# A planned transformer block with its gradients: another order of operations and other homes for the buffers

## The chip, the cores and the metric

The kernel runs on one core of a Trainium2 chip. The metric is the device time of one execution in microseconds (us); lower is better. TensorE is called PE here, VectorE DVE, ScalarE ACT, GpSimd POOL, and SyncE, which issues most transfers, SP.

## The reference

A pre-layernorm block with local attention and a feed-forward part, and then the gradients of its output for all seven inputs, with `grad_out` as the incoming gradient. x is 2048 x 512 in bf16, there are 32 heads of 16, each position attends to 8 positions at distances 0, 2, ... 14, and the feed-forward part is 1792 wide.

```python
def _A_ref(x, wqkv, wo):
    ...
    q, k, v = qkv[0], qkv[1], qkv[2]          # x @ wqkv, by heads
    idx = pos[:, None] - (jnp.arange(W) * dil)[None, :]     # W = 8, dil = 2
    ...
    logits = jnp.einsum("bhsd,bhswd->bhsw", q, kg) * scale
    logits = jnp.where(mask[None, None, :, :], logits, -1e9)
    attn = _softmax(logits, axis=-1)
    o = jnp.einsum("bhsw,bhswd->bhsd", attn, vg)
    return (lambda x, *d: x.transpose(*d))(o, 0, 2, 1, 3).reshape(B, S, D) @ wo

def _B_ref(x, w1, b1, w2, b2):
    h = _gelu(jnp.einsum("bsd,df->bsf", x, w1) + b1)
    return jnp.einsum("bsf,fd->bsd", h, w2) + b2

h = x + _A_ref(_layernorm(x), A_wqkv, A_wo)
h2 = h + _B_ref(_layernorm(h), B_w1, B_b1, B_w2, B_b2)

def reference(A_x, A_wqkv, A_wo, B_w1, B_b1, B_w2, B_b2, B_x, grad_out):
    _out, _vjp = jax.vjp(_f, A_x, A_wqkv, A_wo, B_w1, B_b1, B_w2, B_b2)
    return (_out, *_vjp(grad_out))
```

## The kernel before

**Chunks and stages.** The 2048 rows are worked in four chunks of 512. For each chunk there are three stages.

The first is the attention forward. A layernorm on DVE and ACT gives `ln1`; it is transposed to `ln1T`, multiplied by the q and k halves of wqkv (`wqk`, L802) and by `wv` (L819). For the logits DVE multiplies q with the shifted k, in products of 128 x 4096 elements (`prf`, L672), and PE sums each product over a head's 16 columns with matmuls that put out 32 partitions ("32-column sums", L679). After the softmax, the weighted sum over v works likewise: POOL gathers shifted rows (L661), DVE multiplies (`prbo`, L698), PE sums (`bsum`, L707), and ACT empties the bank into `ost` (the operation "sink", L712). `oT` is its transpose, and wo with the residual gives `h` (L910). A second layernorm gives `ln2`, which goes to memory and comes back transposed as `ln2T` (L559).

The second stage is the feed-forward part, forward and backward. ff1 (L948) makes 14 tiles f0 to f13 of 128 x 512, each in one PSUM bank; ACT empties each bank with the bias added into `xb` (L950), and a gelu over up to four tiles gives `gl` (L953). ff2 (L1004) sums over all 14 tiles, and DVE adds `h` (`h2s`). The derivative of the gelu is made in place by ACT (a square L968, a tanh L972) and DVE (L969 to L982). gg (L1029) multiplies grad_out by w2, tile by tile, each in a bank that DVE empties while it multiplies by the derivative (gh, L1031). ACT makes column sums of grad_out (`jkb`, L1020). gl2 (L1052) goes back through w1, and a layernorm backward gives the gradient of h. Tiles `gl` and gh are also transposed to rows and stored (`g_d`, `gh_d`), for the weight gradients.

The third stage is the attention backward: products and sums of the kind above for the gradients of the logits, v, q and k (`prb`, `prbv`, `prbq`, `prbk`, with gathers `Rv`, `Rq`, `Rk` on POOL), then gl1 (L1165) back through wqkv and the first layernorm backward, which reads `ln1` again (`ln1b`, L1158). The weight gradients (L1193, results `wgs`) read the stored rows back (`gw1in`, `gw2in`) in groups and run where PE is free and at the end.

**The order.** The function calls do not set the order. Each call to `op()` only records an operation with its engine, its buffers and its function in a list of 2029; every buffer, in SBUF or PSUM, is an entry in a list of 969. Then `schedule()` takes two tuples written out in the file: `TURN`, one global order of the 2029 operations, and `HOMES`, a place for each of the 969 buffers: a byte offset in SBUF, or a number from 0 to 7 of a PSUM bank of 512 fp32 columns.

```python
    if len(self.turn) == len(self.ops) and len(self.homes) == len(self.bufs):
        for b, h in zip(self.bufs, self.homes):
            b.home = h
        self.order = [self.ops[i] for i in self.turn]
```

`emit()` issues the operations in that order and gives each buffer its place. An engine carries out its own operations strictly in that order; between engines the program waits where data has to be ready, and also where a place is used again: who writes into a bank waits until the bank's last reader is done. So `HOMES` decides for whom a matmul waits beyond its data, and `TURN` decides what that reader has queued ahead of it on its engine. DMAs are operations of SP or POOL in the same order.

Of the kernel before, what the change touches and what calls it, by code (L numbers as in the profile page):

```python
# [14 lines left out]
ACT = mybir.ActivationFunctionType  # L15
# [412 lines left out]
def kernel(  # L428
# [410 lines left out]
    def p1_attn(c):  # L839
# [15 lines left out]
        op("ACT", 0.61, lambda: A.copy(out=m1h(), in_=m1()[64:128, :]), r=[m1], w=[m1h], tag="m1h")  # L855
        op("DVE", tt_us(512), lambda: V.tensor_tensor(out=m2(), in0=m1()[0:64, :], in1=m1h(), op=ALU.max), r=[m1, m1h], w=[m2], tag="m2")
        op("ACT", 0.61, lambda: A.copy(out=m2h(), in_=m2()[32:64, :]), r=[m2], w=[m2h], tag="m2h")
# [648 lines left out]
)  # L1506
NV = (0, 1, 2, 3)
N2D = ()
B2PE = ()
GB2PE = ()  # L1510
GWA = ()
B1PE = ()
P1_OFF, P3_OFF = 400.0, 0.0
KEEP = 2
RLQ = "SP"
FM1 = ()
FM2 = (0, 1, 2, 3)
EARLY = 1
# [38 lines left out]
```

## Time and profile before

| what | us |
| --- | --- |
| median of 3 runs | 604.17 |
| lowest and highest run | 602.34 and 605.82 |
| the profiled execution, its own time | 603.35 |
| the profiled execution, its span | 601.6 |
| PE, DVE, ACT, POOL busy in the span | 565.8, 492.1, 353.2, 86.6 |
| mean granted TensorE clock | 0.994 |

The span runs from the first to the last instruction; the time of an execution has a little more around it. The busy times are of one profiled execution. In the rows of a timeline stand the start, the duration, the engine, the line of the kernel and the operation with its tiles; what is in brackets at the end is how long the engine stood idle before it, and what ended that. "xN" is the number of instructions that a row holds.

### The profile page before, as it was taken

Reading aid. Unit: us, or ns where it says so; the run is one execution under the profiler, and the core shown is the slowest. Engines: PE = TensorE matmul, PEld = TensorE weight load, DVE = VectorE, ACT = ScalarE, POOL = GpSimd, SP = SyncE. Lnnn points to the kernel's source line nnn. Section 1 sums busy time; section 2 is a strip of 40 time slices with the busy share of each in tenths; the row PEclk is TensorE's granted clock in tenths of the full one; section 3 lists DMA queues with packets and bytes.
Section 4 is the critical chain, followed back from the end, with each engine's and each line's share of the span. In section 5 each row is a group of like instructions: output and inputs, shape, how many; then the busy total and the mean of one; then the engine's idle time right before and its main releaser. Section 6 shows DMA issues by size and latency. Waiting matters only on the chain.

```text
span 601.6 us, 9239 instructions
## 1 busy us (share of the span) xinstructions
PE 565.8 (94%) x3526; PEld 257.4 (43%) x3580; DVE 492.1 (82%) x644; ACT 353.2 (59%) x519; POOL 86.6 (14%) x89
## 2 busy tenths in 40 slices
PE   4999989889879999999999999999999999999997
PEld 2444433434324444444455343334444354444443
DVE  8799899899899989998774679999999998984500
ACT  4578989998993797679545231316535535165112
POOL 3120505021000001000000300223213322100000
PEclk9999999999889999999999999999999999999999
DMA  8258999999998978979997999898898997979312
GB/s 256 86 187 265 331 258 299 262 177 328 238 251 238 281 166 234 211 210 197 277 252 193 285 351 254 259 342 318 289 378 325 338 326 251 333 219 325 108 36 70
DMA packets 161067, 150.46 MB, mean 250 GB/s; under 512 B 110688, under 2 KB 147456, under 8 KB 156160
## 3 DMA queue, kind: packets, MB, share of 16 engines
q1 hardware_dynamic: 154688, 102.69, 63.4%
q0 software_dynamic: 6336, 47.19, 22.0%
q8 instruction: 28, 0.46, 0.3%
q14 instruction: 15, 0.12, 0.1%
HBM read 78.25 MB, written 42.77 MB: 201 GB/s over the span
## 4 chain that ended last, share of the span: by engine, by line
PE 68%; DMA 8%; ACT 7%; DVE 4%; issue 3%; POOL 1%; SPq 0%; DVEq 0%; ACTq 0%; POOLq 0%
PE ps L1193 24%; PE ps L1029 8%; PE ps L1052 7%; PE ps L1165 6%; PE ps L1004 5%; PE ps L948 5%; PE ps L707 4%; PE ps L1074 2%; DMA gw1in<-gh_d 2%; PE ps L722 2%; DMA goT<-in_grad_out_dram 2%; DMA ln2T<-ln 2%; DMA out_dram<-wgs 2%; DVE prbo L698 1%; ACT xb L950 1%
## 5 line engine op out<-in xcount | busy, mean ns | idle before, releaser
L1029 PE MATMUL ps<-goT,w2T 128*128 128x512 bf16 x219 | 56.9, 389 | 8.5 <-ACT ost L712 4.5
L948 PE MATMUL ps<-ln2T,w 128*128 128x512 bf16 x224 | 55.4, 387 | 3.0 <-DMA ln2T<-ln 2.0
L1193 PE MATMUL ps<-gw1in,ln2b 128*128 128x512 bf16 (+1 forms) x256 | 52.7, 353 | 1.2 <-DMA gw1in<-gh_d 1.2
L1004 PE MATMUL ps<-w,gl 128*128 128x512 bf16 x219 | 52.5, 380 | 0.4 <-ACT ost L712 0.2
L1052 PE MATMUL ps<-w1T,xb 128*128 128x512 bf16 x217 | 51.3, 380 | 0.5 <-issue 0.2
L1193 PE MATMUL ps<-gor,gw2in 128*128 128x512 bf16 x217 | 50.7, 380 | 0.5 <-issue 0.2
L1031 DVE SCALAR_TENSOR_TENSOR xb<-xb,ps 128x512 bf16<-128x512 bf16 x56 | 38.1, 684 | 12.6 <-PE ps L1029 11.8
L1165 PE MATMUL ps<-wqkvT,gqkvT 128*128 128x512 bf16 x183 | 43.3, 380 | 0.8 <-issue 0.5
L950 ACT ACTIVATE xb<-ps,b1c 128x512 bf16<-128x512 f32 x56 | 36.9, 688 | 9.3 <-PE ps L948 9.0
L698 DVE TENSOR_TENSOR prbq<-Rq,cfq 128x4096 bf16<-128x4096 bf16 x16 | 36.2, 2286 | 5.1 <-DMA Rq<-k_d,rowi 1.5
L672 DVE TENSOR_TENSOR prb<-got,vw 128x4096 bf16<-128x4096 bf16 x16 | 36.2, 2282 | 4.9 <-PE ps L679 3.1
L737 ACT ACTIVATE gyr<-ps,rstd 128x512 bf16<-128x512 f32 x32 | 22.0, 687 | 31.1 <-PE ps L1165 16.3
L698 DVE TENSOR_TENSOR prbk<-Rk,cfk 128x4096 bf16<-128x4096 bf16 x16 | 36.0, 2285 | 4.6 <-PE ps L707 3.7
L564 ACT CAST wgs<-ps 128x512 bf16<-128x512 f32 (+1 forms) x30 | 16.3, 561 | 38.8 <-PE ps L1193 38.8
L672 DVE TENSOR_TENSOR prf<-qt,kt 128x4096 bf16<-128x4096 bf16 x16 | 36.1, 2274 | 3.4 <-ACT kt L564 3.2
L698 DVE TENSOR_TENSOR prbo<-Ro,cfo 128x4096 bf16<-128x4096 bf16 x16 | 36.4, 2288 | 2.5 <-PE ps L707 1.4
L1029 PEld LDWEIGHTS <-w2T 128*128 128x128 bf16 x224 | 22.0, 99 | 35.6 <-issue 11.3
L698 DVE TENSOR_TENSOR prbv<-Rv,cfv 128x4096 bf16<-128x4096 bf16 x16 | 36.3, 2285 | 0.5 <-ACT wgs L564 0.4
L661 POOL DMA_INDIRECT Rq<-k_d,rowi x8 | 16.4, 2051 | 131.7 <-DMA out_dram<-gbs 106.3
L1193 PEld LDWEIGHTS <-ln2b 128*128 128x128 bf16 x256 | 23.6, 98 | 27.0 <-issue 7.7
L948 PEld LDWEIGHTS <-w 128*128 128x128 bf16 x224 | 21.5, 99 | 31.2 <-issue 7.7
L968 ACT ACTIVATE x<-xb 128x2048 bf16<-128x2048 bf16 (+1 forms) x16 | 27.0, 1690 | 11.7 <-DVE h2s L1006 6.0
(175 smaller groups left out, 1066.6 us busy)
## 6 DMA issues: line engine op xcount, KB each, us to landing
g_d<-xrg SPq DMA_DIRECT2D x12, 512.0 KB
gh_d<-xrh SPq DMA_DIRECT2D x12, 512.0 KB
gw2in<-g_d SPq DMA_DIRECT2D x3, 2048.0 KB
gw1in<-gh_d SPq DMA_DIRECT2D x3, 2048.0 KB
ln_d<-ln SPq DMA_DIRECT2D x8, 512.0 KB
w<-in_B_w_dram SPq DMA_DIRECT2D x2, 1792.0 KB
out_dram<-wgs SPq DMA_DIRECT2D x13, 256.0 KB
v_d<-tmv SPq DMA_DIRECT2D x8, 256.0 KB
```

Of the source, the lines that this page charges most:

```text
L672: op("DVE", tt_us(4096), lambda g=g, pr=pr: V.tensor_tensor(out=pr(), in0=ql()[:, g, :].unsqueeze(1).to_broadcast([P, W, 512]), in1=_sub(k ...
L698: V.tensor_tensor(out=pr().rearrange("p a j (d h) -> p a j d h", h=H), in0=_sub(R()[:, o0, 0:1], [[st, 2], [512, 4], [32, DH], [1, H]]), i ...
L707: T.matmul(ps()[32 * j:32 * j + 32, :], lhsT=S32[:], rhs=pr()[:, hf, j, :], start=(hf == 0), stop=(hf == 1), skip_group_check=True)
L948: T.matmul(ps(), lhsT=w1()[:, dc, f * P:(f + 1) * P], rhs=cols(ln2T[c], dc, c in FM2), start=(dc == 0), stop=(dc == DC - 1))
L950: op("ACT", act_us(512, 1), lambda f=f, ps=ps, xb=xb, f0=f0: A.activation(out=xb()[:, f - f0, :], in_=ps(), func=ACT.Identity, bias=b1c[:, ...
L968: op("ACT", act_us(N), lambda xb=xb, x2=x2: A.activation(out=fl(x2), in_=fl(xb), func=ACT.Square), r=[xb], w=[x2], tag="x2", slack=6000)
L1004: T.matmul(ps(), lhsT=d["g"][f // 4]()[:, f % 4, j * P:(j + 1) * P], rhs=w2()[:, f, :], start=(f == 0), stop=(f == FT - 1))
L1029: T.matmul(ps(), lhsT=w2T()[:, dc, f * P:(f + 1) * P], rhs=goT()[:, dc, :], start=(dc == 0), stop=(dc == DC - 1))
L1031: op("DVE", 0.70, lambda f=f, ps=ps, z=z, f0=f0: V.scalar_tensor_tensor(out=z()[:, f - f0, :], in0=z()[:, f - f0, :], scalar=1.0, in1=ps() ...
L1052: T.matmul(ps(), lhsT=d["d"][f // 4]()[:, f % 4, j * P:(j + 1) * P], rhs=w1T()[:, f, :], start=(f == 0), stop=(f == FT - 1))
L1165: T.matmul(ps(), lhsT=d["gqkv"]()[:, b, j * P:(j + 1) * P], rhs=wqkvT()[:, b, :], start=(i == 0 and b == ks[0]), stop=(i == 2 and b == ks[ ...
L1193: T.matmul(ps()[:, 0:N], lhsT=l, rhs=r, start=(n == 0), stop=(n == k - 1))
```

## The change

Three things change in the file; the list of recorded operations stays the same: 2029 operations and 969 buffers, in both.

- `TURN` is another order of the same 2029 operations. The median operation stands 10 places from where it stood, the mean 18.
- `HOMES` is another list: 716 of 969 buffers have another place, 307 of the 408 PSUM places among them.
- `p1_attn` gets a branch: for chunks in a new tuple `MD` two copies of the softmax's maximum between partitions would be DMAs of SP instead of copies of ACT. `MD` is empty.

The diff, with the two tuples cut to their first lines:

```diff
-        op("ACT", 0.61, lambda: A.copy(out=m1h(), in_=m1()[64:128, :]), r=[m1], w=[m1h], tag="m1h")
+        if c in MD:
+            op("SP", 0.5, lambda: SY.dma_start(out=m1h(), in_=m1()[64:128, :]), r=[m1], w=[m1h], dma=0.25, tag="m1h")
+        else:
+            op("ACT", 0.61, lambda: A.copy(out=m1h(), in_=m1()[64:128, :]), r=[m1], w=[m1h], tag="m1h")
...
-        op("ACT", 0.61, lambda: A.copy(out=m2h(), in_=m2()[32:64, :]), r=[m2], w=[m2h], tag="m2h")
+        if c in MD:
+            op("SP", 0.5, lambda: SY.dma_start(out=m2h(), in_=m2()[32:64, :]), r=[m2], w=[m2h], dma=0.15, tag="m2h")
+        else:
+            op("ACT", 0.61, lambda: A.copy(out=m2h(), in_=m2()[32:64, :]), r=[m2], w=[m2h], tag="m2h")
...
 TURN = (
-    41, 0, 5, 4, 3, 1, 2, 18, 9, 7, 25, 6, 24, 10, 12, 29, 19, 23, 30, 8, 22, 11, 26, 31, 34, 27, 35, 144, 39, 20, 28, 40, 33, 32, 147,
-    37, 36, 145, 38, 146, 48, 148, 265, 149, 49, 266, 42, 50, 263, 43, 150, 153, 51, 44, 152, 154, 52, 151, 76, 155, 158, 53, 45, 159, 46,
...
+    0, 5, 4, 2, 1, 3, 9, 18, 6, 25, 13, 10, 24, 7, 29, 17, 22, 30, 19, 23, 11, 20, 8, 26, 31, 21, 27, 35, 34, 39, 28, 32, 33, 40, 147, 37,
+    144, 38, 145, 48, 146, 49, 148, 263, 149, 42, 50, 265, 43, 150, 153, 51, 44, 154, 152, 45, 151, 41, 76, 52, 46, 53, 58, 78, 47, 156,
...
 HOMES = (
-    32192, 40384, 44480, 85440, 173760, 188096, 99776, 204480, 130624, 114112, 23936, 89536, 165568, 77248, 225088, 52672, 153152, 169664,
-    161472, 212672, 188096, 220992, 208576, 114112, 220992, 212672, 208576, 204480, 0, 200384, 196288, 2, 1, 225088, 188096, 4, 6, 6, 2,
...
+    32192, 40384, 44480, 85440, 173760, 188096, 99776, 134720, 130624, 114240, 23936, 91648, 165568, 77248, 225216, 52672, 153280, 169664,
+    161472, 212672, 188352, 221120, 208576, 114112, 126784, 212672, 208576, 204480, 0, 28032, 23936, 4, 6, 165568, 219968, 4, 6, 0, 0, 6,
...
 B1PE = ()
+MD = ()
```

The operations of which the prediction speaks, in both orders: the excerpt of PE's and of ACT's order around gg f2 of chunk 0 (c is the chunk, f the tile; gg are of chunk 0).

```
before, PE:  gg f10, ff1 c2, ff1 c2, gg f0, gg f11, ff1 c2, ff1 c1, bsum c3, gg f1, ff1 c1, gg f2
after,  PE:  gg f9, gg f7, gg f10, gg f0, gg f11, gg f1, ff1 c1, ff1 c2, ff1 c2, ff1 c1, gg f2, ff1 c2, ff1 c1, bsum c3
before, ACT: xb c2, xb c2, square c1, xb c1, gelu c1, tanh c1, square c1, sink c3, xb c1, gelu c1
after,  ACT: gelu c1, xb c1, xb c2, xb c1, gelu c1, square c0, xb c1, xb c1, gelu c1, sink c3
```

244 rows, old and new, of tables (HOMES, TURN) are left out of this document.

## The prediction

> **What bounds the kernel now.** I read the page first: the busy shares, and the slices, which tell whether the shares are the same everywhere. The profiled execution took 603.35 us, its span 601.6; the 1.75 around the span I leave as it is.
>
> ```profile
> span 601.6 us, 9239 instructions
> ...
> PE 565.8 (94%) x3526; PEld 257.4 (43%) x3580; DVE 492.1 (82%) x644; ACT 353.2 (59%) x519; POOL 86.6 (14%) x89
> ...
> PE   4999989889879999999999999999999999999997
> ...
> DVE  8799899899899989998774679999999998984500
> ACT  4578989998993797679545231316535535165112
> ...
> PEclk9999999999889999999999999999999999999999
> ...
> GB/s 256 86 187 265 331 258 299 262 177 328 238 251 238 281 166 234 211 210 197 277 252 193 285 351 254 259 342 318 289 378 325 338 326 251 333 219 325 108 36 70
> ```
>
> PE bounds the whole, but not every slice. Each digit is 15 us. From the 13th slice on PE shows only nines but for the last one; before it there are eights and a seven, and there ACT and DVE are as full as PE. The change keeps every operation, so a gain can come only from PE's idle time and its granted clock. Next, therefore, the busy time by windows (columns: length, busy time and count of PE, PEld, DVE, ACT, POOL, then granted clock, DMA share, GB/s).
>
> ```profile
> 75.00:125.00 50.00, 45.11 (x338) 19.24 (x340) 45.35 (x45) 46.45 (x61) 10.23 (x8) 1.00 1.10 265
> 125.00:175.00 50.00, 39.33 (x194) 16.68 (x196) 44.63 (x68) 46.45 (x54) 5.64 (x6) 0.93 1.09 253
> 175.00:475.00 300.00, 296.87 (x1773) 133.90 (x1800) 262.13 (x341) 160.78 (x237) 38.83 (x34) 1.00 0.92 268
> 475.00:500.00 25.00, 22.96 (x200) 12.53 (x199) 23.09 (x19) 11.42 (x24) 6.06 (x5) 1.00 0.94 339
> ```
>
> From 75 to 175 PE is idle for 4.89 + 10.67 = 15.56 us; in the 300 us after that only for 3.13; another 2.04 lie in 475 to 500. So the stretch to look at is 75 to 175, where chunk 3's attention runs beside the first feed-forward chunks. What PE waited for there, from the waits view of that window (total, times, longest):
>
> ```profile
> PE ps L1029 <- ACT ost L712: 4.5, 1, 4.5
> PE ps L1029 <- ACT xb L950: 2.5, 1, 2.5
> PE ps L948 <- DMA ln2T<-ln: 2.0, 2, 1.6
> PE ps L910 <- ACT oT L564: 1.6, 1, 1.6
> PE ps L1029 <- ACT rb L564: 1.1, 1, 1.1
> ```
>
> Five rows, 11.7 of the 15.56 us. Three of them are no data waits: gg (L1029) needs nothing from ost, xb or rb. It is given the PSUM bank that ACT is to empty. The timelines of PE and of ACT show the two largest.
>
> ```profile
> 156.69 1.44 PE L1029 MATMUL ps<-goT,w2T 128*128 128x512 bf16 x4 [2.48 <-ACT xb L950]
> ...
> 164.51 0.62 PE L707 MATMUL ps<-prbo,S 128*32 128x512 bf16 x8
> 165.28 0.81 PE L1029 MATMUL ps<-goT,w2T 128*128 128x512 bf16 x3 [0.16 <-issue]
> ...
> 171.47 3.23 PE L1029 MATMUL ps<-goT,w2T 128*128 128x512 bf16 x8 [4.51 <-ACT ost L712]
> ...
> 154.15 1.91 ACT L953 ACTIVATE gl<-xb 128x2048 bf16<-128x2048 bf16 x1
> 155.97 2.40 ACT L950 ACTIVATE xb<-ps,b1c 128x512 bf16<-128x512 f32 x4
> ...
> 165.34 1.91 ACT L953 ACTIVATE gl<-xb 128x2048 bf16<-128x2048 bf16 x1
> 167.22 1.91 ACT L972 ACTIVATE xb<-xb 128x2048 bf16<-128x2048 bf16 x1
> 169.04 1.89 ACT L968 ACTIVATE x<-xb 128x2048 bf16<-128x2048 bf16 x1
> 170.84 0.58 ACT L712 ACTIVATE ost<-ps 128x512 bf16<-128x512 f32 x1
> ```
>
> The banded sums at 164.51 are done at 165.1, but their eviction stands behind a gelu, a tanh and a square of 1.9 us each and ends at 171.4, and the next gg starts at once. In the other case a gelu of 1.91 stands ahead of the evictions. The clock pays a second time:
>
> ```profile
> 157.10:160.50 3.40, 3.40 (x10) 1.19 (x9) 3.40 (x5) 3.37 (x5) 0.00 (x0) 0.51 1.07 232
> ...
> 170.80:174.20 3.40, 2.73 (x7) 0.98 (x7) 3.12 (x4) 3.01 (x6) 0.00 (x0) 0.50 1.04 313
> ```
>
> Around both gaps PE is granted half its clock for 3.4 us: of 3.40 + 2.73 busy us half is lost, 3.0 us.
>
> **The change, part by part.** I compared the order of operations on each engine and the last user of each bank in the two built programs. Operations move by 3 to 5 us on PE, DVE and ACT, and the branch on MD is not taken (MD is empty): nothing.
>
> *The bank waits of gg.* For the 4.51 us: gg f2 of chunk 0 now takes the bank of ff1 f11 of chunk 1, whose eviction is queued behind one gelu instead of three long operations, and the late ost has its bank retaken only nine PE operations on. For the 2.48 and the 1.1: these gg now take banks emptied by gh on DVE. Six gg in a row (f9, f7, f10, f0, f11, f1) hang so on DVE's 0.68 us reads. At worst one product is queued ahead, which costs:
>
> ```profile
> L672 DVE TENSOR_TENSOR prb<-got,vw 128x4096 bf16<-128x4096 bf16 x16 | 36.2, 2282 | 4.9 <-PE ps L679 3.1
> ```
>
> So 8.1 us go, and 1.0 comes back (0 to 2.3; I take the lower half, as in PE's order no single gg has a product just ahead of its gh). For the 2.0 of ln2T, PE has about 5.4 us of ff2 and wo matmuls put between the transposed load and its first use; the first wo there itself waits for an eviction: 0.8 stays (0.3 to 1.2). For the 1.6 of oT, no gelu but one 0.7 us eviction stands ahead of it: 0.4 stays (0 to 0.8). Sum of the five: 11.7 + 3.0 of clock - 2.2 = 12.5 us, if nothing else were in the way.
>
> *ACT and DVE set a floor under that.* In 75 to 175 ACT is busy 92.9 of 100 us and DVE 90.0. PE cannot pull ahead unless they have less to do before the same point of PE's order. Counting what stands ahead of gg's 171.47 position, three column sums (jkb), an xb, a square and a tanh have gone behind it, one other square has come ahead:
>
> ```profile
> L972 ACT ACTIVATE xb<-xb 128x2048 bf16<-128x2048 bf16 x5 | 9.6, 1913 | 0.4 <-DVE xb L971 0.4
> L968 ACT ACTIVATE x<-xb 128x2048 bf16<-128x2048 bf16 x5 | 9.4, 1901 | 0.0
> ...
> L1020 ACT ACTIVATE jkb<-goT 128x512 bf16<-128x512 bf16 x4 | 2.5, 629 | 1.0 <-DMA goT<-in_grad_out_dram 1.0
> ```
>
> 3 x 0.63 + 0.69 + 1.91 + 1.90 - 1.90 = 4.5 us less for ACT; DVE by the same count 1.4 less. At ACT's present share 92.9 - 4.5 = 88.4 us take 95.2: a gain of 4.8. At DVE's present share, (90.0 - 1.4)/0.90 = 98.4: a gain of 1.6. If half of ACT's 7.1 us of idle is used too, 88.4/0.9645 = 91.7: a gain of 8.3. I take ACT's 4.8: the two great stalls are ACT's, and DVE's own idle time there is partly waiting for PE. Bounds 1.6 and 8.3. What was postponed falls after 175, where ACT is busy 160.78 of 300 us: nothing.
>
> *The rule for the clock.* The row above has half a clock after a gap of 2.48 us. The Trainium skill ("TensorE: Matmul & The Clock Gate", Part 1, What's actually happening) states that PE falls to half its clock after at least one idle window of about 3.4 us, the window running freely; the 3.4 us length agrees with this trace, the 2.48 us gap is shorter than its window. By the row the bound of 2.3 for gg's new waits could bring a half-clocked stretch (1.7 more); by the page it could not. At my 1.0 neither does.
>
> *Runs of 32-column sums.* Four fewer changes of shape on PE (76 against 80); entering and leaving costs some 0.16 (the issue row at 165.28): -0.6, between 0 and -0.8.
>
> *The start.*
>
> ```profile
> 3.63 1.05 SPq L550 DMA_DIRECT2D wqk<-in_A_wqkv_dram  x2
> 4.72 0.51 SPq L784 DMA_DIRECT2D xt<-in_A_x_dram  x1
> ...
> 11.30 8.25 PE L802 MATMUL ps<-ln1T,wqk 128*128 128x512 bf16 x24 [1.10 <-ACT ln1T L564]
> ```
>
> SP issues wqk's k half fourth, the q half only after the zero rows and another 512 KB of x, while PE's first products at 11.30 are still q. 512 KB at the 256 GB/s of the first slice are 2.0 us: +0.5, bounds 0 (now they wait for ACT, not for weights) and 2.0.
>
> *SP and POOL later on.* The transposed loads of w2T and w1T are rearranged (the last piece of w2T some 30 us later), still 25 us ahead of use: nothing; without that cover a load's several us each. The load of ln1b for chunk 1 goes 36 us back in PE's order; DVE alone waits for it, in slices where it is at four and five tenths: nothing for PE, up to 8 us at DVE's end, which lies 30 us before PE's. On POOL, eight gathers of attention's backward now stand only 8.4 to 9.8 us of PE work ahead of the product that reads them, and the gathers of 400 to 520 took:
>
> ```profile
>   DVE prbk L698: 0.9, 2
> ...
> DMA to landing us min/median/max: 7.0/10.3/14.2
> ```
>
> Measured so the shortfall is 9.2 us in sum, 2.5 before: up to +6.7 on DVE. Before, of 2.5 only 0.9 was waited for ("who waited for it"), so 0.36 x 6.7 = 2.4 on DVE, and as PE has some work of its own ahead, I take half, +1.2. The weight gradients' wait
>
> ```profile
> L1193 PE MATMUL ps<-gw1in,ln2b 128*128 128x512 bf16 (+1 forms) x256 | 52.7, 353 | 1.2 <-DMA gw1in<-gh_d 1.2
> ```
>
> stays, at about 1.5: its load is issued 2.6 us earlier, used 4 earlier. Together +1.5, bounds 0 and 7.0.
>
> **Sum:** -4.8 - 0.6 + 0.5 + 1.5 = -3.4: 603.35 becomes 599.95. The median of the three runs, 604.17, lies 0.82 above the profiled one: 600.8.
>
> **The rivals.** *DVE is the bound of 75 to 175* (0.28): gg's banks now hang on gh, so PE gains only the 1.6; with -0.6, +0.5 and +1.5 this is -0.2: 604.0 (603.2 if the late costs are half). For it: DVE's nines in those slices. Against it: 4.5 us of stall that DVE had no part in.
>
> *The gathers come late* (0.25, the one that ends slower): from 400 to 500 DVE is at nines, PE loses what DVE loses, and the whole 6.7 is paid, with the gain of 75 to 175 at 1.6: -1.6 - 0.6 + 0.5 + 7.0 = +5.3, 609.5; with half the price 606. It decides once gathers take above 9 us from issue to landing, which the median of 10.3 already does. Against it: only 0.9 us was waited for before.
>
> *The gaps close fully* (in the forecast's 0.47, its low end): PE is let off to the 8.3 and the late costs are nothing: -8.3 - 0.6 = -8.9, 595.3.
>
> *The change does nothing*, both orders being equal in effect, is within the first rival.
>
> **How the numbers follow.** The likeliest is 600.8, its own range 595.3 to 603. The range reaches up into the gathers' rival at a little over its half price: 595 to 607.5; beyond are some 0.05 below and 0.13 above. About 0.5%, 3.0 us, can be told from no change. The forecast lies just beyond that line (601.15) on the fast side. Faster by more than that: 0.47, the forecast. Same: 0.28, the DVE case. Slower by more: 0.25.
>
> **What would show it.** Right: in the waits of PE from 75 to 175 the rows of ost and xb with 4.5 and 2.5 are gone, no half clock remains, and PE's idle time there falls from 15.6 to about 10, with ACT still above nine tenths. Wrong, towards the first rival: gg waits for gh in that window, in about the sum that went. Wrong, towards the second: prbk, prbv and prbq (L698) wait for gathers for over 4 us between 400 and 520, and PE's idle time from 400 to 500 rises above 5. Wrong at the start: the first L802 waits for wqk. All my steps would fail if PE's busy time itself moved by more than 3.6 us, the 0.6 and the 3.0 of clock.

## The result and the profile after

| | kernel before | changed kernel |
| --- | --- | --- |
| median of 20 runs, us | 604.29 | 603.27 |
| lowest and highest, us | 601.46 and 619.72 | 592.89 and 611.68 |
| ratio to the kernel before, 95% interval | | 0.9909, 0.988 to 0.9939 |

The ratio counts the runs within 1.5 per cent of each kernel's fastest; of the changed kernel only 8 of 20 lie there, because its times are spread evenly over 19 us. So the change gains 0.9 per cent by the ratio, and next to nothing by the median of all runs. With the first 604.17 the ratio stands for 598.7 us; 600.8 was forecast. A second set (run 1 below) gave 1.0007, 0.9962 to 1.0051, and a median of 607.56 against 602.68: no gain.

The page of the changed kernel shows what is behind it. Lines of the code after `p1_attn` are 6 higher than before: ff1 is L954, gg L1035, gh L1037, the weight gradients L1199.

```profile
span 610.0 us, 9218 instructions
...
PE   3999999998069999999999999799999999999997
...
PEclk9999999999579999999999999999999999999999
...
GB/s 263 74 214 321 266 274 344 213 271 140 62 200 261 268 219 310 181 271 200 307 218 227 258 397 263 287 213 328 357 316 293 316 332 297 257 244 315 150 87 52
```

Where the kernel before had eights and a seven from the 6th to the 12th slice, PE is now at nines, but for a hole that begins in the 10th slice and fills the 11th and half of the 12th, at half clock; in the 10th and 11th the DMA engines move 140 and 62 GB/s, where they moved 328 and 238. The waits of PE from 75 to 175 us:

```profile
PE ps L954 <- DMA ln2T<-ln: 22.3, 2, 22.0
PE ps L916 <- ACT h L564: 0.9, 1, 0.9
```

All five rows of the prediction (ost, xb, ln2T, oT, rb; 11.7 us) are gone or at most 0.3, and one new wait of 22 us has come. The timelines of SP, POOL and PE around it:

```profile
137.62 7.71 SPq L559 DMA_TRANSPOSE w1T<-in_B_w_dram  x1
145.44 25.29 SPq L559 DMA_TRANSPOSE ln2T<-ln  x1
...
138.29 1.13 POOL L661 DMA_INDIRECT Ro<-v_d,rowi  x1 [0.31 <-ACT x L974]
...
172.94 4.06 PE L954 MATMUL ps<-ln2T,w 128*128 128x512 bf16 x12 [22.03 <-DMA ln2T<-ln]
```

A piece of w1T's transposed load starts 0.7 us before POOL issues a gather, and takes 7.7 us; ln2T of chunk 2 is issued when its data is ready and takes 25.3, where the other ln2T took 1.9 to 2.3. That gather is as slow, the longest of those of 85 to 200 us (from issue to landing):

```profile
DMA to landing us min/median/max: 7.0/8.8/32.2
```

In the changed order PE has ff1 of chunk 2 directly behind that ln2T, and nothing else to do.

### The profile page after: what moved, and what is told of

Read it like the earlier page. It is cut to its first block, busy times and chain, and to the rows that moved or that the text cites. A ratio compares the mean times of both kernels' runs of the same rounds, so it can differ in the third digit from the quotient of the medians.

```text
span 610.0 us, 9218 instructions
## 1 busy us (share of the span) xinstructions
PE 561.1 (92%) x3526; PEld 256.4 (42%) x3580; DVE 490.0 (80%) x644; ACT 353.3 (58%) x519; POOL 94.1 (15%) x89
## 5 line engine op out<-in xcount | busy, mean ns | idle before, releaser
L954 PE MATMUL ps<-ln2T,w 128*128 128x512 bf16 x224 | 54.5, 387 | 22.3 <-DMA ln2T<-ln 22.3
L1035 PE MATMUL ps<-goT,w2T 128*128 128x512 bf16 x217 | 53.4, 379 | 1.3 <-DMA goT<-in_grad_out_dram 0.6
L1199 PE MATMUL ps<-gw1in,ln2b 128*128 128x512 bf16 (+1 forms) x256 | 53.3, 353 | 0.0
L1199 PE MATMUL ps<-gor,gw2in 128*128 128x512 bf16 x216 | 51.5, 380 | 0.5 <-issue 0.2
L1037 DVE SCALAR_TENSOR_TENSOR xb<-xb,ps 128x512 bf16<-128x512 bf16 x56 | 37.8, 684 | 14.3 <-PE ps L1035 13.4
L954 PEld LDWEIGHTS <-w 128*128 128x128 bf16 x224 | 21.4, 99 | 49.4 <-DMA ln2T<-ln 22.5
L661 POOL DMA_INDIRECT Rq<-k_d,rowi x8 | 19.9, 2490 | 119.0 <-PE ps L1010 103.8
L672 DVE TENSOR_TENSOR prf<-qt,kt 128x4096 bf16<-128x4096 bf16 x16 | 35.8, 2277 | 2.7 <-ACT kt L564 2.5
L1199 PEld LDWEIGHTS <-ln2b 128*128 128x128 bf16 x256 | 23.6, 98 | 24.2 <-issue 5.1
L1035 PEld LDWEIGHTS <-w2T 128*128 128x128 bf16 x224 | 21.6, 98 | 27.5 <-issue 1.9
L1058 PEld LDWEIGHTS <-xb 128*128 128x128 bf16 x224 | 21.7, 98 | 26.3 <-issue 0.6
```

Source lines behind the costliest of these rows:

```text
L661: G.indirect_dma_start(out=R().rearrange("p a d -> p (a d)"), out_offset=None, in_=_ap(t[0:1, :], [[10 * D, RB // 10], [1, 10 * D]]), in_o ...
L672: op("DVE", tt_us(4096), lambda g=g, pr=pr: V.tensor_tensor(out=pr(), in0=ql()[:, g, :].unsqueeze(1).to_broadcast([P, W, 512]), in1=_sub(k ...
L954: T.matmul(ps(), lhsT=w1()[:, dc, f * P:(f + 1) * P], rhs=cols(ln2T[c], dc, c in FM2), start=(dc == 0), stop=(dc == DC - 1))
L1035: T.matmul(ps(), lhsT=w2T()[:, dc, f * P:(f + 1) * P], rhs=goT()[:, dc, :], start=(dc == 0), stop=(dc == DC - 1))
L1037: op("DVE", 0.70, lambda f=f, ps=ps, z=z, f0=f0: V.scalar_tensor_tensor(out=z()[:, f - f0, :], in0=z()[:, f - f0, :], scalar=1.0, in1=ps() ...
L1058: T.matmul(ps(), lhsT=d["d"][f // 4]()[:, f % 4, j * P:(j + 1) * P], rhs=w1T()[:, f, :], start=(f == 0), stop=(f == FT - 1))
```

## The experiments

**1. The changed kernel again.** No edit.

> The changed kernel unaltered, for a profile and as the base of the next two. Over 20 runs its spans went from 591.2 to 610.0 us, and span = 590.3 + 0.92 x (time at half clock), the time at half clock being 2 x (1 - mean clock) x span. Theory (one wait of varying length): the spans again spread over 10 us or more, on the same line within 4 us, and the profile shows one wait of PE for ln2T of chunk 2 near 151 us, of about the length by which the span exceeds 589. Rival (the spread has many places, such as the gathers after 400 us): the wait for ln2T is about the same in every run, and the rest varies.

Measured: 599.01 to 613.81 us in 12 runs, median 607.56, ratio 1.0007 (0.9962 to 1.0051). The spans of the 12 runs lie within 3.0 us of the line that the first 20 gave. The profile (span 602.1):

```profile
138.73 10.52 SPq L559 DMA_TRANSPOSE w1T<-in_B_w_dram  x1
149.36 12.89 SPq L559 DMA_TRANSPOSE ln2T<-ln  x1
...
164.34 3.98 PE L954 MATMUL ps<-ln2T,w 128*128 128x512 bf16 x9 [12.32 <-DMA ln2T<-ln]
```

```profile
138.00:142.00 4.00, 3.95 (x25) 2.08 (x25) 3.96 (x7) 4.00 (x6) 3.37 (x5) 1.00 1.08 281
142.00:146.00 4.00, 3.47 (x17) 1.49 (x16) 3.72 (x9) 4.00 (x5) 0.00 (x0) 1.00 1.18 177
...
150.00:154.00 4.00, 1.97 (x9) 0.70 (x8) 3.77 (x9) 4.00 (x6) 0.00 (x0) 1.00 1.18 78
154.00:158.00 4.00, 0.00 (x0) 0.00 (x0) 2.27 (x3) 2.96 (x3) 0.00 (x0) 0.56 1.18 49
```

The second rows are windows; the last three columns are the granted clock, the DMA share and GB/s. The wait is 12.3 us here and 22.0 there, and the spans differ by 7.9: the theory, one wait of varying length. That it is this wait is seen in the two profiles; of the other runs only span and clock are known. While it lasts the DMA engines are marked busy throughout, and move 49 to 78 GB/s instead of 281.

**2. The piece of w1T later.** The only edit is in SP's order:

```diff
-w1T (505), ln2T c2 (381), xrg (601), ln2 store (379)
+ln2T c2 (381), xrg (601), ln2 store (379), w1T (505)
```

> The changed kernel with one transposed load, the last piece of w1T (operation 505), moved on SP from just ahead of POOL's gather and of ln2T of chunk 2 to behind both and two more DMAs. Theory (a gather and a transposed load that start together hold each other up for up to 25 us): the gather has the DMA engines to itself, ln2T takes 2 to 6 us, PE's wait of 22 falls below 4, no run is above 595, median 590 to 593. Rival (ln2T is late for its own sake, as it was issued only when its data came, at 145.4, with w1T just done): it still takes above 10 us, and the times are as in the first run of this call.

Measured: 590.91 to 595.10 in 6 runs, median 592.63, ratio 0.9831 (0.9793 to 0.9868).

```profile
145.06 3.21 SPq L559 DMA_TRANSPOSE ln2T<-ln  x1
...
150.29 1.86 SPq L559 DMA_TRANSPOSE w1T<-in_B_w_dram  x1
```

```profile
142.00:146.00 4.00, 3.47 (x17) 1.49 (x16) 3.75 (x8) 3.98 (x6) 0.00 (x0) 1.00 0.88 301
```

The same loads take 3.2 and 1.9 us, the throughput from 142 to 146 us is 301 GB/s instead of 177, PE's wait for ln2T is down to 0.7 us and the spread to 4.2. One operation moved in an order of 2029 is worth 15 us of the median (607.56 to 592.63). The highest run is 0.1 above the bound of 595.

**3. The other partner taken away.** The gather of chunk 3 becomes a memset, all else as in 1:

```diff
+            if tag == "o" and sc == 0 and d_b is v_d[3]:
+                G.memset(R(), 0.0)
+                return
```

> The changed kernel with one of the 32 gathers left out: the first gather of attention's forward in chunk 3 (operation 453) is a memset of its buffer on POOL, so that part of the result is made from zeros. Order and all other DMAs stay. Theory (gather against transposed loads): the piece of w1T at 137.6 takes 2 to 3 us instead of 7.7, ln2T about 2 to 3 instead of 25, and all runs lie at 588 to 593. Rival (the transposed loads or SP's queue alone are slow here, without the gather): PE's wait for ln2T stays above 5 us and the runs still spread.

Measured: 595.32 to 597.48 in 6 runs, median 596.45, ratio 0.9887 (0.9851 to 0.9924).

```profile
138.44 2.63 SPq L559 DMA_TRANSPOSE w1T<-in_B_w_dram  x1
...
149.06 1.92 SPq L559 DMA_TRANSPOSE ln2T<-ln  x1
...
138.86 4.38 POOL L661 MEMSET Ro<- 128x5120 bf16 x1
...
139.33 4.45 DVE L978 TENSOR_SCALAR ga<-x 128x2048 bf16<-128x2048 bf16 x1
```

With w1T's piece at its place but no gather, both transposed loads are quick and the spread is gone. So the long wait takes both. That the times lie 3.8 us above run 2 and above the expected 593 fits the memset: beside it DVE's `ga` took 4.45 us instead of 0.69, PE then waited 3.4 us for gh (L1038 to L1040 in this file), 0.5 in run 2, and 6.8 us at half clock followed, with none in run 2.

**4. The same pair brought together in the kernel before.**

```diff
-h2 store (549), q store (428), h2 store (558), w1T (505)
+w1T (505), h2 store (549), q store (428), h2 store (558)
```

> The kernel before, with the same piece of w1T moved the other way on SP: ahead of three stores, so that it starts within 1 us of the gather of chunk 3 (131.4 us) instead of 4 us after it. Theory (they hold each other up when they start together): the piece takes far above 9 us in at least some runs, ln2T of chunk 2 (151.6 before) and the products of chunk 3 are late, and the time is 5 to 20 us longer, with a spread. Rival (order on SP's queue is harmless, only the queue's length counts): 604 within 1.5, as before.

Measured: 600.11 to 619.01 in 13 runs, median 604.46, against 602.68 for the kernel before; ratio 1.0005 (0.9972 to 1.0039). Five of 13 runs are above 607, and 4 of 23 of the kernel before. In the profile:

```profile
139.19 6.88 SPq L559 DMA_TRANSPOSE w1T<-in_B_w_dram  x1
...
105.76 15.83 SPq L559 DMA_TRANSPOSE goT<-in_grad_out_dram  x1
```

The pair was issued within 0.4 us (the gather at 139.52) and the piece took 6.9, no more than in the kernel before (8.9): a miss for the theory as I wrote it. But the two did not move at the same time: by the trace's records of DMA packets the gather's rows, packets of 10,240 bytes, moved from 147.5 to 155.5 us, when the piece was done. Another transposed load, goT, met another gather (issued at 102.29, packets from 107.8 to 121.3) and took 15.8, where it had taken 7.9; right behind, PE waited 6.9 us in one place, from 118.3 to 125.2. This profile is of the longest run, 619.01; whether the kernel before's own longest runs (618 to 620 in 3 of 20) are of this kind, no trace shows.

The packet records tell the meetings apart in part. ln2T moves in packets of 256 bytes. While the gather of chunk 3 was in flight, 2027 such packets were sent in the changed kernel's first profile (29.0 us from the gather's first packet to its last) and 1712 in run 1 (19.1 us). In the kernel before there were none (5.4 us), and in run 2 380, all at the very end (6.6 us). So in the slow meetings the two kinds alternate, and in these quick ones they follow each other. That is not the whole condition: beside goT in the kernel before, 703 were sent during a gather that took 5.9 us. What makes one such meeting cost 2 us and another 25 is not settled by these runs.

**5. Three banks alone.** The kernel before with three entries of `HOMES`:

```diff
-psg f2: bank 4   psg f10: bank 6   psg f7: bank 7
+psg f2: bank 2   psg f10: bank 3   psg f7: bank 5
```

> The kernel before with three numbers of HOMES changed and its order untouched: the banks of gg f2, f10 and f7 of chunk 0, which PE waited 4.5, 2.5 and 1.1 us for, become banks whose last reader is long done (the eviction after gg f0, that of ff1 f2 of chunk 1, and gh of f5). Theory (these waits are PE's own loss, and ACT catches up in its idle time): the three rows go from the waits of 75 to 175, no half clock is left there, and the time falls by 5 to 11 us, to 592 to 598. Rival (the prediction's floor: ACT has as much to do before the same place as it had, so PE only waits elsewhere): new waits for ACT of 5 us or more in that window, a gain of at most 3.5 us.

Measured: 599.82 to 614.06 in 12 runs, median 603.06 against 602.77 for the kernel before, ratio 0.9976 (0.9947 to 1.0004): no gain that could be told. The waits of PE from 75 to 175, and then the first row of those from 175 on:

```profile
PE ps L1029 <- DMA goT<-in_grad_out_dram: 4.4, 1, 4.4
PE ps L948 <- ACT xb L950: 2.1, 3, 1.5
PE ps L948 <- DMA ln2T<-ln: 1.7, 1, 1.7
PE ps L910 <- ACT oT L564: 1.4, 1, 1.4
...
PE ps L1193 <- DMA gw1in<-gh_d: 2.8, 1, 2.8
```

```profile
161.76 3.26 SPq L559 DMA_TRANSPOSE xrh<-xb  x1
165.19 1.91 SPq L559 DMA_TRANSPOSE goT<-in_grad_out_dram  x1
```

The three rows did go, but not the half clock (170.0 to 173.4 us). gg f2 is followed in PE's order by the first gg of chunk 1. Its goT starts on SP when the transposed load of xrh ahead of it has ended, and is under way until 167.1; PE goes on at 169.3. Up to 475 us PE was busy for 4.0 us more than in the kernel before; it gave most of that back at the weight gradients, where the wait for gw1in grew from 1.2 to 2.8 and a stretch of half clock followed (granted clock 0.93 from 475 to 500, 1.00 before). Both statements were half right: PE waited elsewhere, as the rival said, but for transfers (4.4) more than for ACT (xb from 0.6 to 2.1).

**6. The start put right.** Run 2, and besides

```diff
-SP: wqk k half (6), zero rows, x of chunk 2, wqk q half (7);  PE: b1 (20), ln transposes
+SP: wqk q half (7), zero rows, x of chunk 2, wqk k half (6);  PE: ln transposes, b1 (20)
```

> The changed kernel with w1T's last piece moved as in the second run, and the start as before: the q half of wqk loaded ahead of the k half, and the transpose of b1 with its copy behind the first layernorm's transposes and norms. Theory (the start costs 1.2 us, by the first product with wqk at 12.5 us instead of 11.3): 591.4, 1.2 below the second run's 592.6, and the first product at 11.3 or earlier. Rival (what is won at the start is lost again at the next wait, as DVE and ACT are full up to 160 us): within 0.5 us of 592.6.

Measured: median 591.01 (589.73 to 593.71, 6 runs), ratio 0.9798 (0.9756 to 0.984). The first product with wqk, in the changed kernel's first profile and here:

```profile
12.52 3.85 PE L802 MATMUL ps<-ln1T,wqk 128*128 128x512 bf16 x11 [1.94 <-DMA wqk<-in_A_wqkv_dram]
```

```profile
10.65 8.97 PE L802 MATMUL ps<-ln1T,wqk 128*128 128x512 bf16 x32 [0.99 <-ACT ln1T L564]
```

1.9 us earlier here; with the changed start the other profiles have 12.05 (run 1) and 11.80 (run 2), with the old one 11.17 (run 7). In the medians it is 1.6, in the theory's sense; but runs 2 and 6 are of two sets, and the two intervals overlap. In the same profile a wait stands out that the kernel before had not:

```profile
365.13 0.07 DVE L1340 MEMSET glf<- 128x16 uint32 x1 [6.30 <-DMA shk<-glf]
...
369.64 1.05 PE L707 MATMUL ps<-prbq,S 128*32 128x512 bf16 x8 [2.97 <-DVE prbq L698]
```

The change had put this memset behind loads that read the same tile, one of them behind a transposed load of 5.95 us on SP.

**7. That memset earlier.** Run 6 with operation 1191 moved:

```diff
-DVE: glf c1 (1272) ... glf c0 (1220), product, memset (1191), cfq
+DVE: glf c1 (1272), memset (1191) ... glf c0 (1220), product, cfq
```

> The sixth kernel with one more operation moved: the memset of glf's last columns on DVE (operation 1191) goes from behind three of the four loads shk that read glf to just behind the first write of glf, nearly where the kernel before has it. Theory (in the sixth run DVE stood 6.3 us for those loads, as the fourth of them was queued on SP behind a transposed load, and PE then waited 3.0 us for prbq at 369.6): DVE's wait and PE's wait of 3.0 go, and the time falls by 1 to 3 us, to 588 to 590. Rival (PE makes the 3.0 up at a later wait, such as for the gathers after 400 us): within 0.5 us of 591.0.

Measured: 586.36 to 588.67 in 5 runs, median 586.91 against 604.52 for the kernel before, ratio 0.9716 (0.9691 to 0.9741). This is the fastest version, 2.8 per cent below the kernel before. The median is 4.1 below that of run 6, more than the 1 to 3 expected: behind PE's wait of 3.0, run 6 had 3.4 us at half clock (369.5 to 372.9), which the expectation left out. PE's waits for prbq shrink to 0.5 us in all, and the clock is whole:

```profile
359.33 2.10 DVE L687 STREAM_TRANSPOSE cfq<-glf 128x512 bf16<-128x512 bf16 x2
```

```profile
75.00:125.00 50.00, 46.69 (x340) 19.79 (x342) 48.75 (x47) 48.26 (x62) 7.13 (x8) 1.00 1.05 268
125.00:175.00 50.00, 46.16 (x228) 20.66 (x232) 47.14 (x83) 45.05 (x53) 3.80 (x5) 1.00 1.07 258
```

## Why the prediction was right, and where it was wrong

The range held, and by the ratio the direction, but that 600.8 came near was luck: it came out of two errors against each other. The gain was put too small, and a loss was not seen. In the second set there was no gain at all.

*The signs.* Of those for the changed kernel only the first came true, the rows of ost and xb. Its half clock did not go (155.1 to 175.6 us), PE's idle time from 75 to 175 rose to 26.2 us and ACT fell to 78.2 of 100, as the new wait lies there. In run 2, without that wait, they hold: from 75 to 162.6 PE is idle for 7.1 us at the whole clock, and ACT is busy for 84.3 of 87.6. The last sign came true against the prediction: PE's busy time moved by 4.7 us (565.8 to 561.1), and in run 2 by 5.7, more than the 3.6 allowed; what is known of that stands under "What stays open".

*The bank waits.* The step held: the rows of ost and xb went, gg waits at most 0.5 us for gh (1.0 was forecast, 0 to 2.3), oT and ln2T of chunk 1 nearly nothing. In run 2, where PE is not held up ahead of it, gg f2 still waits 1.7 us for an xb.

*The floor set by ACT, -4.8 (1.6 to 8.3),* is the step that was mis-sized. Run 2 shows the change without the new wait. Windows from 75 us to the start of gg f2 of chunk 0, in the kernel before (which starts it at 171.47) and in run 2 (at 155.89):

```profile
75.00:171.47 96.47, 80.91 (x520) 34.61 (x524) 87.24 (x109) 89.76 (x111) 15.88 (x14) 0.98 1.09 259
```

```profile
75.00:155.89 80.89, 73.86 (x478) 32.18 (x483) 78.23 (x100) 77.64 (x95) 11.17 (x13) 1.00 1.09 262
```

ACT has 12.1 us less ahead of it, not 4.5, because gg f2 itself moved and much of ACT's work with it (and 7.0 us of PE's), and ACT's share rose from 0.930 to 0.960. I had counted at a fixed place of PE's order and held the share. What was won is read from the waits: the listed ones of PE in 75 to 175 add to 15.2 us before and to 6.7 in run 2 (75 to 162.6); with the 3.0 of clock that is 11.5, above the bound of 8.3 and close to the 12.5 that the prediction had "if nothing else were in the way". In run 5, with the order as it was, other banks alone bring nothing that can be told; but PE stood there for goT and not for ACT, so that run does not show ACT as the floor. That the order did it along with the homes is argued: the new order with the old banks was not run.

*The clock.* No half clock is left in runs 2 and 7 but in the last 1.1 us (mean 0.999 and 1.000). The Trainium skill ("TensorE: Matmul & The Clock Gate", Part 1, What's actually happening) has it that PE falls to half after at least one idle window of about 3.4 us. That it falls after idling the traces show, but a wait of 2.48 us in the kernel before and one of 2.97 in run 6 were enough. Over the 20 runs the time at half clock, 2 x (1 - mean clock) x span, goes from 1 to 22 us and the span follows it within 4 us, 590.3 + 0.92 times it.

*Changes of shape, -0.6.* The price of 0.16 was read from the gap at 165.28, and that reading is wrong: gg is four matmuls and that row has three, so the gap is a record that is missing. In run 2 the gg behind the same sums has its four and no gap. No run shows what a change of shape costs.

*The start, +0.5 (0 to 2.0):* right by the bounds. PE's first product with wqk came 0.5 to 1.2 us later than before (11.80 to 12.52 against 11.30) and waited for wqk, 1.9 to 2.3 us, which the last part of the prediction had named as the sign of a wrong step; undoing it gave 1.6 in the medians of two sets.

*The late gathers, +1.2 in a term of +1.5,* were put too high for PE. What DVE waited for from 350 to 520 us in run 7, where the memset is out of the way:

```profile
DVE prbv L698 <- DMA Rv<-go_d,rowi: 6.2, 2, 5.8
DVE prbq L698 <- DMA Rq<-k_d,rowi: 3.6, 2, 2.2
DVE prbk L698 <- DMA Rk<-q_d,rowi: 1.6, 2, 1.4
```

DVE stood 11.4 us for gathers, even more than the 6.7 of the upper bound, but PE's waits for prbq are 0.5 in all and none for prbk is listed. From 400 to 500 us PE is busy for 98.6 us in run 7 and for 97.6 in the kernel before. So the second rival, that PE loses what DVE loses, is refuted, although its sign on DVE came true. The first, with DVE as the bound of 75 to 175, fell with the waits there.

*What was missed.* "SP and POOL later on" looked at whether each transfer is issued early enough before its use, at the duration that it had before. ln2T of chunk 2 passed that: 2 us, and the piece of w1T was nobody's concern, being used much later. That a transposed load and a gather can hold each other up when they meet had its signs in the trace of before, where goT took 7.88 and w1T 8.92 us beside gathers; I took them for queueing. And the memset of run 7 is the kind of wait that the prediction meant to look for, another reader of the same place ahead in another queue, in a tile that I did not check.

*What stays open.* Of the 12.4 us between the spans of run 2 and of the kernel before, PE's idle time explains 6.7 (35.8 to 29.1): the listed waits of 75 to 175 shrank by 8.5, the others grew by 1.8. The other 5.7 are PE's busy time (565.8 to 560.1, with as many records in both): 3.0 by the clock, and of the remaining 2.7 the products with wqk alone (L802) have 2.1, 32.4 to 30.3. The prediction had no term for these, and no run tells why they became shorter.

Open too is what decides whether a transposed load and a gather that meet hold each other up.

## What to carry to other kernels

A transfer that is far ahead of its use still costs if it meets another: when an order is changed, look at which transposed loads and gathers are in flight together, and keep the ones that are in no hurry away from the one that PE waits for next. A stall at a full engine is worth what comes next late: three banks alone gave nothing, the new banks and order together 10 us in the medians, once the meeting was out of the way (602.68 to 592.63). When times of one kernel spread more than another's, compare the granted clock of the runs: here it told the span within 4 us, without a trace of each run.

## What the hardware showed that was not expected

A transposed load and an indirect gather whose packets alternated moved 49 to 78 GB/s together (run 1, 150 to 158 us), with all DMA engines marked busy, and the load took 12.9 and 25.3 us in two profiles; the gather alone ran at 301 (run 2, 142 to 146 us). Not every such meeting is that slow: in the kernel before 703 of the small packets fell in a gather of 5.9 us. The Trainium skill ("DMA: Bandwidth & Descriptors", Rules for kernel authors) says that a transpose next to ordinary DMAs needs nothing. For the time this case shows otherwise: 25.29 us for ln2T against 1.92 without the gather. While a memset of 128 x 5120 ran on POOL (4.38 us), a tensor_scalar on DVE that takes 0.69 us took 4.45 (run 3, one instance).
